# Batch 0 of a sparse attention and MLP kernel: local q, k and v cast in flight, attended tiles normalised in pairs, first weights queued early

## The chip, the cores and the metric

One core of a Trainium2 chip. The metric is the device time of one execution in microseconds, median of several executions. Five engines work side by side: TensorE (matmuls), VectorE, ScalarE, GpSimd, and SyncE, which here only issues transfers. Loads issued by SyncE go through the "hardware queue" and keep their type; loads issued by GpSimd go through the "software queue" and here cast float32 to bf16 in flight.

## The reference

```python
def _attn_ref(q, k, v):                      # q, k, v: (8, 8, 576, 64) float32
    scores = scale * np.matmul(q, k.transpose(0, 1, 3, 2))
    rel = pos[:, None] - pos[None, :]
    mask_local = (rel >= 0) & (rel < 32)                       # heads 0 to 3
    mask_strided = (rel >= 0) & (pos[None, :] % 32 == pos[:, None] % 32)   # heads 4 to 7
    ...                                       # masked softmax over the keys
    return np.matmul(attn, v)

def _moe_ref(x, w_in, w_out):                # x: (4608, 512), w_in: (512, 2048), w_out: (2048, 512)
    h = x @ w_in
    sp = np.where(h > 20.0, h, np.log1p(np.exp(np.minimum(h, 20.0))))
    return ((h * np.tanh(sp)) @ w_out).astype(np.float32)
# reference: x is the attention output, its heads side by side
```

## The kernel before

The parts that the change and the argument touch, with cuts. Heads 0 to 3 are called local, 4 to 7 strided. An "attended tile" is the attention output of 96 queries (local) or 72 (strided) for four heads. A "block" is 512 rows of x going through the MLP: its first half multiplies by w_in, its second by w_out. A "gate" is a tiny transfer on SyncE's queue; what is behind it is asked for only after the gate's source is written.

```python
# helpers: hardware queue (issued by SyncE) in float32, software queue (issued by GpSimd) casting to bf16
def load_qk_loc(b):                           # local k, q: 96 partitions x 6 rows, hardware queue
    for dst, src in ((kl32, k), (ql32, q)):
        nc.sync.dma_start(...)
def load_v_loc(b): ...                        # local v: 5 loads of 256-byte rows, hardware queue
def load_w_in(c0, c1):                        # 512 columns of w_in each, cast in flight
    for c in range(c0, c1):
        nc.gpsimd.dma_start(...)

# the prologue: attention of batch 0, cut
load_v_str(0); load_qk_loc(0); load_v_loc(0)
for p in P_s + P_l:
    Po.memset(p[:], 0.0)
...                                           # strided k, q: cast, transpose
cast(Po, vs[0][...], vs32[0:PN])
load_w_in(0, 1)
a.qk("s", 0, Dv); a.qk("s", 1, Dv, True)      # scores, exp, mask
cast_qk_loc(0, Dv, Po)
a.qk("s", 2, Dv, True)
load_w_in(1, 2)
...                                           # local v cast by Po; local k, q transposed; local scores
for j in range(8):
    a.pv("s", j)                              # attended tile, normalised alone by VectorE
a.mask("l", 2, Dv)
load_w_in(2, 4)
load_qk_str(1)
load_w_out(0, 2)
nc.sync.dma_start(gate[:], x_s[0:1, 5, :])    # SyncE's queue waits here, then asks for batch 1
load_qk_loc(1)
load_v(1)
...
cast_qk_loc(1, Po, Po)                        # GpSimd, in this order
cast_v(1, Po, Po)
load_w_out(2, 4)
load_qk_str(2)
for t in range(NBLK):                         # block t: MLP half 1 and transposes of batch t+1,
    ...                                       # then MLP half 2 and attention of batch t+1
            if t == 0:
                for n in {3: (4, 5), 4: (6, 7), 6: (0, 1), 7: (2, 3)}.get(i, ()):
                    ts[n]()                   # 0 to 3: strided k, q; 4 to 7: local k, q of batch 1
```

The softmax here doesn't subtract the row's maximum and nothing guards it: scores larger than these inputs give would overflow.

Of the kernel before, what the change touches and what calls it, by code (L numbers as in the profile page):

```python
# [37 lines left out]
def kernel(ctx, tc, q, k, v, moe_w_in, moe_w_out, out):  # L38
# [52 lines left out]
    def tile_t(name):  # L91
        return ps_t.tile([128, 512], F32, tag="pt", name=name)
# [8 lines left out]
    def load_qk_loc(b):  # L101
        for dst, src in ((kl32, k), (ql32, q)):
            nc.sync.dma_start(
                dst[0:PL].rearrange("p h j d -> p h (j d)"),
                src[b, 0:4].rearrange("h (p j) d -> p h (j d)", j=CL),
            )
# [30 lines left out]
    def cast(eng, out_, in_):  # L137
        if eng is nc.scalar:
            nc.scalar.copy(out_, in_)  # L139
        else:  # L140
            eng.tensor_copy(out_, in_)  # L141
# [11 lines left out]
    def t_step(b, kind, which, hp, eng=None):  # L153
# [13 lines left out]
        else:  # L167
# [10 lines left out]
                tr[:, 0:S].rearrange("c (j p) -> c p j", j=CL),  # L178
            )

    T_ORDER = [(kd, w, hp) for kd in ("s", "l") for hp in range(2) for w in ("k", "q")]

    def t_steps(b):
# [7 lines left out]
    class Attn:  # L191
# [40 lines left out]
                op=ALU.mult,  # L232
            )

        def pv(self, kind, i):
            po = tile_t("po")[:, 0:4 * (D + 1)].rearrange("p (h d) -> p h d", h=4)
            for h in range(4):
                if kind == "l":
                    n, m, rhs = 128, WQ, vl[self.b % 2][:, i, h, :]
                    pt, c0 = P_l[i // 2][:, h % 2], WQ * (2 * (h // 2) + i % 2)  # L240
                else:
                    n, m, rhs = PN, PN, vs[self.b % 2][0:PN, h, i, :]
                    job, u = S_AT[i // 2, h]
                    pt, c0 = P_s[job][:, i % 2], PN * u
                nc.tensor.matmul(  # L245
                    po[:, h, :], lhsT=pt[0:n, c0:c0 + 128], rhs=rhs,
                    start=True, stop=True,
                )
            dst = (x_l if kind == "l" else x_s)[0:m, i, :]
            rden = small.tile([128, 4], F32, tag="rden", name="rden")  # L250
            nc.vector.reciprocal(rden[0:m, :], po[0:m, :, D])  # L251
            nc.vector.tensor_tensor(  # L252
                out=dst.rearrange("p (h d) -> p h d", h=4), in0=po[0:m, :, 0:D],
                in1=rden[0:m, :].unsqueeze(2).to_broadcast([m, 4, D]), op=ALU.mult,
            )

        def xt(self, kind, hf, eng=None):
# [52 lines left out]
    def mlp1(t):  # L310
        gT = g_pool.tile([128, 16, 512], BF16, tag="gT", name="gT")

        def group(g):
            ps = ps_mm.tile([128, 2, 512], F32, tag="mm", name="psh")
            for u in range(2):
                fc = 2 * g + u
                for a, n, o in segs(t):
                    for cc in range(4):
                        nc.tensor.matmul(  # L319
                            ps[:, u, o:o + n], lhsT=w_in[:, cc, fc * 128:(fc + 1) * 128],  # L320
                            rhs=xT[:, cc, a:a + n], start=(cc == 0), stop=(cc == 3),
                        )
            nc.scalar.activation(gT[:, 2 * g:2 * g + 2, :], ps[:], AF.Mish)  # L323
        return gT, [lambda g=g: group(g) for g in range(8)]

    def mlp2(t, gT, fc_major=False):
# [22 lines left out]
    with tc.manual_schedule():  # L349
        Po, Dv, Sc = nc.gpsimd, nc.vector, nc.scalar  # L350
        Sc.preload_act_table(AF.Exp)
        Sc.dma_start(consts[:], consts_h.ap())
        st0 = []
        for src in (k, q):
            st = g_pool.tile([128, 16, 512], BF16, tag="gT", name="st0")
            st = st[:].rearrange("p a b -> p (a b)").bitcast(F32)[0:PN, 0:4 * CS * D]
            st = st.rearrange("p (h x) -> p h x", h=4)
            for hp in range(2):
                h = 2 * hp
                nc.sync.dma_start(  # L360
                    st[:, h:h + 2, :],
                    src[0, 4 + h:6 + h].rearrange("h (p j) d -> p h (j d)", j=CS),
                )
            st0.append(st)
        load_v_str(0)
        load_qk_loc(0)
        load_v_loc(0)
        Dv.memset(kTs[:, 16 * PN:16 * PN + 64], 0.0)
        Dv.memset(kTl[:, :, 0:32], 0.0)
        Dv.memset(vl32[0:32, 0, :, :], 0.0)  # L370
# [2 lines left out]
            Dv.memset(vl[i][:, :, :, D:D + 1], 1.0)  # L373
        for i in range(2):
            Dv.memset(vl[i][0:32, 0, :, D:D + 1], 0.0)
        for p in P_s + P_l:
            Po.memset(p[:], 0.0)

        a = Attn(0)
        for hp in range(2):  # L380
            h = 2 * hp
            cast(Dv, ks[0][0:PN, h:h + 2, :], st0[0][:, h:h + 2, :])
            t_step(0, "s", "k", hp, Dv)
        cast(Dv, qs[0][0:PN, 0:2, :], st0[1][:, 0:2, :])
        t_step(0, "s", "q", 0, Sc)
        cast(Sc, qs[0][0:PN, 2:4, :], st0[1][:, 2:4, :])
        t_step(0, "s", "q", 1, Sc)
        cast(Po, vs[0][0:PN, :, :, 0:D], vs32[0:PN])
        load_w_in(0, 1)
        a.qk("s", 0, Dv)  # L390
        a.qk("s", 1, Dv, True)
        cast_qk_loc(0, Dv, Po)
        a.qk("s", 2, Dv, True)
        load_w_in(1, 2)
        for i in range(0, NW, 3):
            cast(Po, vl[0][:, i:i + 3, :, 0:D], vl32[:, i:i + 3, :, :])
        for hp in range(2):
            t_step(0, "l", "k", hp, Dv)
            t_step(0, "l", "q", hp, Sc)
        a.qk("l", 0, Po)  # L400
        a.qk("l", 1, Po, True)
        a.qk("l", 2, None, True)
        for j in range(8):
            a.pv("s", j)
        a.mask("l", 2, Dv)
        load_w_in(2, 4)
        load_qk_str(1)
        load_w_out(0, 2)
        nc.sync.dma_start(gate[:], x_s[0:1, 5, :])
        load_qk_loc(1)  # L410
        load_v(1)
        for i in range(3):
            a.pv("l", i)
        a.xt("s", 0)
        a.xt("s", 1)
        for i in range(3, 6):
            a.pv("l", i)
        a.xt("l", 0)
        a.xt("l", 1)
        cast_qk_loc(1, Po, Po)  # L420
        cast_v(1, Po, Po)
        load_w_out(2, 4)
# [5 lines left out]
            load_v(2)  # L428

        for t in range(NBLK):  # L430
            gT, g1 = mlp1(t)
            ts = t_steps(t + 1) if t + 1 < B else []
            at = attn_steps(t + 1) if t + 1 < B else []
            if t == 0:
                at[8].append(load_next)
            for i, g in enumerate(g1):
                g()
                if t == 0:
                    for n in {3: (4, 5), 4: (6, 7), 6: (0, 1), 7: (2, 3)}.get(i, ()):
                        ts[n]()  # L440
                elif i < len(ts):
                    ts[i]()
            if t + 3 < B:
                load_qk_str(t + 3)
            for i, g in enumerate(mlp2(t, gT, fc_major=(t == 0))):
                g()
                if i < len(at):
                    for s in at[i]:
                        s()
            if t + 2 < B:  # L450
                cast_qk_loc(t + 2, Po, Po)
                cast_v(t + 2, Po, Po)
            if t + 3 < B:
                load_qk_loc(t + 3)
                load_v(t + 3)
# [30 lines left out]
```

## Time and profile before

| | before |
|---|---|
| time, median (range) of three executions | 348.3 us (347.7 to 348.6) |
| span in the profile | 345.9 us |
| TensorE busy | 315.6 us, 91% |
| first MLP matmul | 34.28 us |
| second half of block 0 starts | 51.99 us |
| block 1 starts | 72.15 us |
| each later block | 35.45 us |

The page of a kernel gives busy times, a picture of 40 equal slices in tenths, and groups of instructions. The chain of waits follows the last instruction back to what released it, step by step (start, duration, what). A timeline lists one engine's instructions: start, duration, engine, line, operation, what it writes and reads, and in square brackets how long the engine had been idle and on what. "PE" is TensorE, "POOL" GpSimd, "SPq" SyncE's queue. In the names, `kl`, `ql`, `vl` are local k, q, v, `ks`, `qs`, `vs` strided ones, `lq` the new bf16 buffer of batch 0's local k and q, `psh` and `pso` the results of the MLP's two halves. The lines that carry the reading are in the prediction below.

Two lines more are wanted later: on GpSimd's timeline of the kernel before, batch 1's local k and q are cast as they land.

```profile
32.11 1.46 POOL L141 CAST kl<-kl 96x1536 bf16<-96x1536 f32 x1 [0.19 <-DMA kl<-in_k_dram]
...
37.42 1.47 POOL L141 CAST ql<-ql 96x1536 bf16<-96x1536 f32 x1 [3.85 <-DMA ql<-in_q_dram]
```

Local k landed about 32.1 us and local q at 37.4, with TensorE needing them after 42 us.

### The profile page before, as it was taken

How to read it: one execution, taken by the hardware profiler on the slowest of the kernel's cores; microseconds unless marked ns; L12 is line 12 of the kernel's file. 1: busy time of each engine (PE TensorE's matmuls, PEld its weight loads, DVE VectorE, ACT ScalarE, POOL GpSimd, SP SyncE). 2: the span in 40 equal slices, each digit the busy share in tenths (PEclk: the TensorE clock that was granted, in tenths of full speed). 3: DMA queues.
4: the chain of work that ended last, by engine and by line, in shares of the span. 5: the costliest groups of instructions: out<-in, count | busy, mean ns of one | idle time of the engine just before them, and what ended most of it. 6: DMA issues, size and time to landing. Idle time of an engine off the chain costs nothing.

```text
span 345.9 us, 6447 instructions
## 1 busy us (share of the span) xinstructions
PE 315.6 (91%) x2737; PEld 171.2 (49%) x2784; DVE 115.3 (33%) x315; ACT 174.8 (51%) x191; POOL 116.1 (34%) x101
## 2 busy tenths in 40 slices
PE   1366999999999999999999999999999999999993
PEld 1244454555455545554569655544555454444441
DVE  3356044523462236233632363236423540000000
ACT  1543447275646464656465645665466637414511
POOL 5368215726292109310941086007700600000000
PEclk9999999999999999999999999999999999999999
DMA  6997993999993961299119810960110011011011
GB/s 182 206 172 175 225 178 59 189 214 245 223 198 92 227 106 62 64 221 140 63 41 246 138 37 27 244 110 1 63 63 0 2 63 61 0 63 61 0 63 61
DMA packets 48573, 39.63 MB, mean 115 GB/s; under 512 B 26656, under 2 KB 41056, under 8 KB 48544
## 3 DMA queue, kind: packets, MB, share of 16 engines
q1 hardware_dynamic: 38576, 30.81, 38.7%
q0 software_dynamic: 9824, 8.33, 15.3%
q8 instruction: 22, 0.36, 0.5%
q10 hardware_dynamic: 144, 0.08, 0.1%
q14 instruction: 7, 0.06, 0.1%
HBM read 38.09 MB, written 9.44 MB: 137 GB/s over the span
## 4 chain that ended last, share of the span: by engine, by line
PE 72%; DMA 8%; SPq 5%; DVE 5%; issue 3%; ACT 3%; POOL 3%; POOLq 0%; ACTq 0%
PE psh L319 32%; PE pso L334 28%; PE po L245 4%; DMA ql<-in_q_dram 4%; DMA vl<-in_v_dram 4%; SPq L117 4%; DVE x_s L252 2%; PE tr L170 2%; PE tr L161 2%; PE ps L202 2%; ACT Ps L220 2%; DVE qTl L141 1%; PE ps L213 1%; PE trx L275 1%; PE trx L265 1%
## 5 line engine op out<-in xcount | busy, mean ns | idle before, releaser
L334 PE MATMUL pso<-w_out,gT 128*128 128x512 bf16 x546 | 136.9, 379 | 1.5 <-issue 0.2
L319 PE MATMUL psh<-xT,w_in 128*128 128x512 bf16 (+1 forms) x623 | 134.0, 360 | 1.8 <-ACT xT L139 0.7
L323 ACT ACTIVATE gT<-psh 128x1024 bf16<-128x1024 f32 x72 | 73.7, 1024 | 56.0 <-PE psh L319 54.6
L319 PEld LDWEIGHTS <-w_in 128*128 128x128 bf16 x640 | 60.3, 99 | 55.5 <-issue 3.6
L334 PEld LDWEIGHTS <-gT 128*128 128x128 bf16 x576 | 49.0, 97 | 44.3
L139 ACT COPY xT<-trx 128x576 bf16<-128x576 bf16 x32 | 20.4, 639 | 47.8 <-PE trx L275 31.8
L229 POOL TENSOR_TENSOR Ps<-Ps,consts_sb 72x576 bf16<-72x576 bf16 x7 | 8.9, 1275 | 90.0 <-ACT Ps L220 90.0
L229 POOL TENSOR_TENSOR Pl<-Pl,consts_sb 128x768 bf16<-128x768 bf16 x23 | 37.1, 1641 | 1.4 <-ACT Pl L220 1.3
L341 ACT COPY osb<-pso 128x1024 f32<-128x1024 f32 x18 | 18.2, 1012 | 27.4 <-PE pso L334 27.4
L251 DVE RECIPROCAL rden<-po 72x4 f32<-72x4 f32 (+1 forms) x112 | 19.8, 176 | 36.5 <-PE po L245 36.4
L252 DVE TENSOR_TENSOR x_s<-po,rden 72x256 bf16<-72x256 f32 x64 | 26.9, 420 | 2.2
L220 ACT ACTIVATE Pl<-ps 128x768 bf16<-128x768 f32 x24 | 19.2, 811 | 14.0 <-PE ps L202 14.0
L220 ACT ACTIVATE Ps<-ps 72x864 bf16<-72x864 f32 (+1 forms) x24 | 19.1, 806 | 7.4 <-PE ps L213 6.6
L141 DVE COPY kTl<-tr 128x576 bf16<-128x576 bf16 x16 | 12.1, 758 | 29.8 <-PE tr L170 29.8
L252 DVE TENSOR_TENSOR x_l<-po,rden 96x256 bf16<-96x256 f32 x48 | 20.2, 421 | 1.7
L141 POOL CAST vs<-vs 72x2048 bf16<-72x2048 f32 x8 | 15.2, 1896 | 12.9 <-DMA vs<-in_v_dram 12.9
L229 DVE TENSOR_TENSOR Ps<-Ps,consts_sb 72x864 bf16<-72x864 bf16 (+1 forms) x17 | 10.6, 622 | 26.3 <-ACT Ps L220 26.3
L141 DVE COPY kTs<-tr 128x576 bf16<-128x576 bf16 x16 | 7.3, 458 | 34.8 <-PE tr L161 34.8
L245 PE MATMUL po<-vs,Ps 72*128 72x65 bf16 x256 | 17.2, 201 | 1.8 <-DVE x_s L252 0.9
L141 POOL CAST vl<-vl 128x768 bf16<-128x768 f32 x16 | 12.8, 831 | 15.1 <-DMA vl<-in_v_dram 15.1
L245 PE MATMUL po<-vl,Pl 128*128 128x65 bf16 x192 | 14.6, 200 | 3.3 <-DVE rden L251 2.5
L245 PEld LDWEIGHTS <-Ps 72*128 72x128 bf16 x256 | 12.2, 101 | 8.4 <-DVE x_s L252 3.7
(47 smaller groups left out, 211.1 us busy)
## 6 DMA issues: line engine op xcount, KB each, us to landing
out_dram<-osb SPq DMA_DIRECT2D x18, 512.0 KB, 3.1
vl<-in_v_dram SPq DMA_DIRECT2D x32, 160.0 KB, 9.2
vs<-in_v_dram SPq DMA_DIRECT2D x8, 576.0 KB
kl<-in_k_dram SPq DMA_DIRECT2D x8, 576.0 KB, 8.4
ql<-in_q_dram SPq DMA_DIRECT2D x8, 576.0 KB, 8.5
w_in<-in_moe_w_in_dram POOLq DMA_DIRECT2D x4, 512.0 KB, 8.7
w_out<-in_moe_w_out_dram POOLq DMA_DIRECT2D x4, 512.0 KB, 14.5
ks<-in_k_dram POOLq DMA_DIRECT2D x7, 288.0 KB, 12.1
```

What stands on the lines that cost most here:

```text
L117: nc.sync.dma_start(vl32[:, 1:NW, h, :], win)
L139: nc.scalar.copy(out_, in_)
L141: eng.tensor_copy(out_, in_)
L220: nc.scalar.activation(pt[0:n, :, 0:nw], ps[0:n, :, 0:nw], AF.Exp, scale=scale)
L229: meng.tensor_tensor(out=pm, in0=pm, in1=mk[0:n, :].unsqueeze(1).unsqueeze(1).to_broadcast([n, 2, nu, w]), op=ALU.mult,)
L245: nc.tensor.matmul(po[:, h, :], lhsT=pt[0:n, c0:c0 + 128], rhs=rhs, start=True, stop=True,)
L251: nc.vector.reciprocal(rden[0:m, :], po[0:m, :, D])
L252: nc.vector.tensor_tensor(out=dst.rearrange("p (h d) -> p h d", h=4), in0=po[0:m, :, 0:D], in1=rden[0:m, :].unsqueeze(2).to_broadcast([m, ...
L319: nc.tensor.matmul(ps[:, u, o:o + n], lhsT=w_in[:, cc, fc * 128:(fc + 1) * 128], rhs=xT[:, cc, a:a + n], start=(cc == 0), stop=(cc == 3),)
L323: nc.scalar.activation(gT[:, 2 * g:2 * g + 2, :], ps[:], AF.Mish)
L334: nc.tensor.matmul(p[:, ot % 2, :], lhsT=gT[:, fc, 128 * ot:128 * ot + 128], rhs=w_out[:, fc, :], start=(fc == 0), stop=(fc == 15),)
L341: nc.scalar.copy(osb[:], p[:])
```

## The change

Its intent is to start the MLP earlier. Local q, k and v of batch 0 are cast by the transfer and no longer by engines; q and k go to partitions 64 to 127. All four chunks of w_in are queued right behind them. VectorE normalises two attended tiles at a time. The first two groups of the MLP begin with the half of their contraction that is ready first. The gate for batch 1 now waits for the third chunk of w_in, and the transposes of batch 1 move later: the local ones by two groups, one of the strided ones by one.

```diff
+    def t_step_loc0(src, dst, hp, eng):       # 64x64 transposes from partitions 64 to 127
+        tr = tile_t("tr")[:].bitcast(BF16)
+        for j in range(9):
+            for e in range(2):
+                nc.tensor.transpose(
+                    tr[64 * e:64 * e + 64, 64 * j:64 * j + 64], src[64:128, 2 * hp + e, j, :],
+                    ident[64:128, 64:128],
+                )
+        cast(eng, ...)
 ...
+        def pv2(self, kind, i, from_mm=False): # two attended tiles, one reciprocal, one multiply
+            po = tile_s(from_mm)[:, :, 0:4 * (D + 1)].rearrange("p e (h d) -> p e h d", h=4)
+            for e in range(2):
+                self.pv_mm(kind, i + e, po[:, e])
+            ...
 ...                                           # mlp1(0): groups 0 and 1 split in two halves of the contraction
-        load_qk_loc(0)
-        load_v_loc(0)
-        for p in P_s + P_l:
+        for p in P_s:
+            Dv.memset(p[:], 0.0)
+        for p in P_l[0:2]:
             Po.memset(p[:], 0.0)
+        load_loc0(kl0, k)                      # Po.dma_start: cast in flight
+        Po.memset(P_l[2][:], 0.0)
+        load_loc0(ql0, q)
+        Po.dma_start(vl[0][32:128, 0, :, 0:D], ...)
+        for h in range(4):
+            Po.dma_start(vl[0][:, 1:NW, h, 0:D], win)
+        load_w_in(0, 4)
 ...
-        load_w_in(0, 1)  / load_w_in(1, 2) / load_w_in(2, 4), cast_qk_loc(0, ...), casts of vl
-        for j in range(8):
-            a.pv("s", j)
+        a.pv2("s", 0) ... a.pv2("s", 2, True) ... a.pv("s", 4); a.pv("s", 5) ... a.pv2("s", 6)
         load_qk_str(1)
         load_w_out(0, 2)
-        nc.sync.dma_start(gate[:], x_s[0:1, 5, :])
+        nc.sync.dma_start(gate[:], w_in[0:1, 0, 1024:1280])
 ...
-                    for n in {3: (4, 5), 4: (6, 7), 6: (0, 1), 7: (2, 3)}.get(i, ()):
+                    for n in {5: (4, 5), 6: (6, 7, 0), 7: (1, 2, 3)}.get(i, ()):
```

More of the change, by code (lines that the diff above doesn't have):

```diff
@@ L179, in t_step @@
             )
+    def t_step_loc0(src, dst, hp, eng):
[6 more added lines that the diff above has]
+                )
+        cast(
+            eng, dst.rearrange("c (p j) -> c p j", j=9),
+            tr[:, 0:S].rearrange("c (j p) -> c p j", j=9),
+        )
     T_ORDER = [(kd, w, hp) for kd in ("s", "l") for hp in range(2) for w in ("k", "q")]
@@ L233, in mask, with pv_mm @@
             )
-        def pv(self, kind, i):
-            po = tile_t("po")[:, 0:4 * (D + 1)].rearrange("p (h d) -> p h d", h=4)
+        def pv_mm(self, kind, i, po):
             for h in range(4):
                 if kind == "l":
-                    n, m, rhs = 128, WQ, vl[self.b % 2][:, i, h, :]
+                    n, rhs = 128, vl[self.b % 2][:, i, h, :]
                     pt, c0 = P_l[i // 2][:, h % 2], WQ * (2 * (h // 2) + i % 2)
                 else:
-                    n, m, rhs = PN, PN, vs[self.b % 2][0:PN, h, i, :]
+                    n, rhs = PN, vs[self.b % 2][0:PN, h, i, :]
                     job, u = S_AT[i // 2, h]
@@ L248, in pv @@
                 )
+        def pv(self, kind, i):
+            po = tile_t("po")[:, 0:4 * (D + 1)].rearrange("p (h d) -> p h d", h=4)
+            m = WQ if kind == "l" else PN
+            self.pv_mm(kind, i, po)
             dst = (x_l if kind == "l" else x_s)[0:m, i, :]
@@ L254, in pv @@
                 in1=rden[0:m, :].unsqueeze(2).to_broadcast([m, 4, D]), op=ALU.mult,
+            )
+        def pv2(self, kind, i, from_mm=False):
+            po = tile_s(from_mm)[:, :, 0:4 * (D + 1)].rearrange("p e (h d) -> p e h d", h=4)
+            m = WQ if kind == "l" else PN
+            for e in range(2):
+                self.pv_mm(kind, i + e, po[:, e])
+            dst = (x_l if kind == "l" else x_s)[0:m, i:i + 2, :]
+            rden = small.tile([128, 2, 4], F32, tag="rden2", name="rden2")
+            nc.vector.reciprocal(rden[0:m], po[0:m, :, :, D])
+            nc.vector.tensor_tensor(
+                out=dst.rearrange("p e (h d) -> p e h d", h=4), in0=po[0:m, :, :, 0:D],
+                in1=rden[0:m].unsqueeze(3).to_broadcast([m, 2, 4, D]), op=ALU.mult,
             )
@@ L311, in mlp1, with group @@
         gT = g_pool.tile([128, 16, 512], BF16, tag="gT", name="gT")
-        def group(g):
-            ps = ps_mm.tile([128, 2, 512], F32, tag="mm", name="psh")
+        held = {}
+        def group(g, ccs=(2, 3, 0, 1)):
+            if g not in held:
+                held[g] = ps_mm.tile([128, 2, 512], F32, tag="mm", name="psh")
+            ps = held[g]
             for u in range(2):
@@ L317, in group @@
                 for a, n, o in segs(t):
-                    for cc in range(4):
+                    for cc in ccs:
                         nc.tensor.matmul(
                             ps[:, u, o:o + n], lhsT=w_in[:, cc, fc * 128:(fc + 1) * 128],
-                            rhs=xT[:, cc, a:a + n], start=(cc == 0), stop=(cc == 3),
+                            rhs=xT[:, cc, a:a + n], start=(cc == 2), stop=(cc == 1),
                         )
-            nc.scalar.activation(gT[:, 2 * g:2 * g + 2, :], ps[:], AF.Mish)
+            if ccs[-1] == 1:
+                nc.scalar.activation(gT[:, 2 * g:2 * g + 2, :], ps[:], AF.Mish)
+        if t == 0:
+            return gT, [lambda g=g, c=c: group(g, c) for c in ((2, 3), (0, 1)) for g in range(2)] + [
+                lambda g=g: group(g) for g in range(2, 8)
+            ]
         return gT, [lambda g=g: group(g) for g in range(8)]
@@ L352 @@
         Sc.dma_start(consts[:], consts_h.ap())
-        st0 = []
-        for src in (k, q):
-            st = g_pool.tile([128, 16, 512], BF16, tag="gT", name="st0")
-            st = st[:].rearrange("p a b -> p (a b)").bitcast(F32)[0:PN, 0:4 * CS * D]
-            st = st.rearrange("p (h x) -> p h x", h=4)
-            for hp in range(2):
-                h = 2 * hp
+        st0 = g_pool.tile([128, 16, 512], BF16, tag="gT", name="st0")
+        st0 = st0[:].rearrange("p a b -> p (a b)").bitcast(F32)[0:PN]
+        st0 = [st0[:, 2048 * i:2048 * i + 2048].rearrange("p (h x) -> p h x", h=4) for i in range(2)]
+        for st, src in zip(st0, (k, q)):
+            for h in (0, 2):
                 nc.sync.dma_start(
@@ L363, with load_loc0 @@
                 )
-            st0.append(st)
         load_v_str(0)
-        load_qk_loc(0)
-        load_v_loc(0)
+        lq0 = g_pool.tile([128, 16, 512], BF16, tag="gT", name="lq0")
+        lq0 = lq0[:].rearrange("p a b -> p (a b)")
+        kl0, ql0 = [
+            lq0[:, 2304 * i:2304 * i + 2304].rearrange("p (h j d) -> p h j d", h=4, j=9) for i in range(2)
+        ]
+        def load_loc0(dst, src):
+            Po.dma_start(
+                dst[64:128].rearrange("p h j d -> p h (j d)"),
+                src[0, 0:4].rearrange("h (p j) d -> p h (j d)", j=9),
+            )
         Dv.memset(kTs[:, 16 * PN:16 * PN + 64], 0.0)
@@ L375 @@
             Dv.memset(vl[i][0:32, 0, :, D:D + 1], 0.0)
-        for p in P_s + P_l:
+        Dv.memset(vl[0][0:32, 0, :, 0:D], 0.0)
+        for p in P_s:
+            Dv.memset(p[:], 0.0)
+        for p in P_l[0:2]:
             Po.memset(p[:], 0.0)
+        load_loc0(kl0, k)
+        Po.memset(P_l[2][:], 0.0)
+        load_loc0(ql0, q)
+        Po.dma_start(vl[0][32:128, 0, :, 0:D], v[0, 0:4, 0:96, :].rearrange("h p d -> p h d"))
+        for h in range(4):
+            win = bass.AP(
+                v.tensor, v[0, h:h + 1, WQ - 32:WQ, :].offset, [[D, 128], [WQ * D, NW - 1], [1, D]]
+            )
+            Po.dma_start(vl[0][:, 1:NW, h, 0:D], win)
+        load_w_in(0, 4)
         a = Attn(0)
@@ L382 @@
             cast(Dv, ks[0][0:PN, h:h + 2, :], st0[0][:, h:h + 2, :])
-            t_step(0, "s", "k", hp, Dv)
-        cast(Dv, qs[0][0:PN, 0:2, :], st0[1][:, 0:2, :])
-        t_step(0, "s", "q", 0, Sc)
-        cast(Sc, qs[0][0:PN, 2:4, :], st0[1][:, 2:4, :])
-        t_step(0, "s", "q", 1, Sc)
-        cast(Po, vs[0][0:PN, :, :, 0:D], vs32[0:PN])
-        load_w_in(0, 1)
-        a.qk("s", 0, Dv)
-        a.qk("s", 1, Dv, True)
-        cast_qk_loc(0, Dv, Po)
-        a.qk("s", 2, Dv, True)
-        load_w_in(1, 2)
-        for i in range(0, NW, 3):
-            cast(Po, vl[0][:, i:i + 3, :, 0:D], vl32[:, i:i + 3, :, :])
-        for hp in range(2):
-            t_step(0, "l", "k", hp, Dv)
-            t_step(0, "l", "q", hp, Sc)
-        a.qk("l", 0, Po)
-        a.qk("l", 1, Po, True)
-        a.qk("l", 2, None, True)
-        for j in range(8):
-            a.pv("s", j)
-        a.mask("l", 2, Dv)
-        load_w_in(2, 4)
+            t_step(0, "s", "k", hp, Sc)
+        for hp in range(2):
+            h = 2 * hp
+            cast(Dv, qs[0][0:PN, h:h + 2, :], st0[1][:, h:h + 2, :])
+            t_step(0, "s", "q", hp, Sc)
+            t_step_loc0(kl0, kTl[:, hp, 32:32 + S], hp, Sc)
+        cast(Dv, vs[0][0:PN, :, :, 0:D], vs32[0:PN])
+        for i in range(3):
+            a.qk("s", i, Dv if i < 2 else None, i > 0)
+        for hp in range(2):
+            t_step_loc0(ql0, qTl[:, hp, :], hp, Sc)
+        a.pv2("s", 0)
+        a.mask("s", 2, Dv)
+        a.qk("l", 0, None, True)
+        a.pv2("s", 2, True)
+        a.mask("l", 0, Dv)
+        a.pv("s", 4)
+        a.pv("s", 5)
+        a.qk("l", 1, Po, True)
+        a.qk("l", 2, Po, True)
+        a.pv2("s", 6)
         load_qk_str(1)
         load_w_out(0, 2)
-        nc.sync.dma_start(gate[:], x_s[0:1, 5, :])
+        nc.sync.dma_start(gate[:], w_in[0:1, 0, 1024:1280])
         load_qk_loc(1)
         load_v(1)
-        for i in range(3):
-            a.pv("l", i)
+        gT, g1 = mlp1(0)
         a.xt("s", 0)
         a.xt("s", 1)
-        for i in range(3, 6):
-            a.pv("l", i)
+        a.pv2("l", 0)
+        a.pv2("l", 2, True)
+        g1[0]()
+        a.pv("l", 4)
+        a.pv("l", 5)
         a.xt("l", 0)
+        g1[1]()
         a.xt("l", 1)
+        g1 = g1[2:]
         cast_qk_loc(1, Po, Po)
@@ L430 @@
         for t in range(NBLK):
-            gT, g1 = mlp1(t)
+            if t > 0:
+                gT, g1 = mlp1(t)
             ts = t_steps(t + 1) if t + 1 < B else []
```

## The prediction

> **What bounds the kernel now.** I read the page's rows first, then the chain of waits up to 75 us, then GpSimd's timeline across the one long transfer on that chain, then stretches by engine, then the DMA queues by window. From the page of the kernel before:
>
> ```profile
> span 345.9 us, 6447 instructions
> PE 315.6 (91%) x2737; PEld 171.2 (49%) x2784; DVE 115.3 (33%) x315; ACT 174.8 (51%) x191; POOL 116.1 (34%) x101
> ...
> PE   1366999999999999999999999999999999999993
> ...
> DMA  6997993999993961299119810960110011011011
> ```
>
> TensorE is idle for 345.9 - 315.6 = 30.3 us, nearly all in the first four of 40 slices (8.65 us each): the attention of batch 0, before any MLP matmul can run. The timeline puts the first MLP matmul at 34.28 us, the first matmul of the second MLP half of block 0 at 51.99, and the start of block 1 at 72.15. After that a block takes 107.74 - 72.29 = 35.45 us, and the next 35.45 again, at TensorE's pace. Only the time before 72.15 can shrink. The DMA row is full there as well, but for a gap just before slice 4. The stretches say the same:
>
> ```profile
> 34.00:52.00 18.00, 17.39 (x118) 8.76 (x121) 3.73 (x7) 9.01 (x10) 3.36 (x2) 1.00 1.15 203
> 52.00:72.20 20.20, 19.09 (x206) 10.03 (x207) 10.61 (x32) 10.40 (x13) 11.95 (x12) 1.00 0.82 137
> ...
> 89.80:107.70 17.90, 17.21 (x184) 9.32 (x187) 9.25 (x30) 8.94 (x12) 12.30 (x9) 1.00 0.85 156
> ```
>
> (columns: PE, PEld, DVE, ACT, POOL busy, clock, DMA share, GB/s). The second half of block 0 takes 20.2 us where block 1's takes 17.9: something holds TensorE up by some 2 us. The chain of waits names it:
>
> ```profile
> 27.15 0.57 SPq L103
> ...
> 37.67 4.31 SPq L117
> 42.02 13.27 DMA vl<-in_v_dram
> 55.43 0.94 POOL vl L141 x2
> ```
>
> So what sets the end is not the late start of the MLP. It is the local v of batch 1, requested behind k and q of batch 1 from 27.15 us on and complete at about 55.4. GpSimd, whose queue is in order, is stuck behind it:
>
> ```profile
> 55.43 1.60 POOL L141 CAST vl<-vl 128x768 bf16<-128x768 f32 x2 [10.82 <-DMA vl<-in_v_dram]
> 56.98 1.50 POOL L132 DMA_DIRECT2D w_out<-in_moe_w_out_dram  x2
> 58.45 0.76 POOL L97 DMA_DIRECT2D ks<-in_k_dram  x1
> 59.17 0.75 POOL L97 DMA_DIRECT2D qs<-in_q_dram  x1
> ...
> 61.30 1.32 POOL L229 TENSOR_TENSOR Ps<-Ps,consts_sb 72x576 bf16<-72x576 bf16 x1
> ```
>
> After the cast it issues six loads, and only at 61.30 masks the last strided scores of batch 1. The mask ends at 62.62, 7.2 us after the landing. TensorE's next attention product starts at 62.67, and block 0 ends 9.5 us later. There are thus two chains into 72.15: the MLP's start plus its work, and the landing of v plus 7.2 + 9.5 = 16.7 us.
>
> **What the Trainium skill says.** "DMA: Bandwidth & Descriptors", section "Issuing engines are not separate DMA queues": loads issued by any engine run on the same 16 DMA engines and interleave. The trace agrees: from 28 to 55.4 us the software queue takes 58.8% of the engines and the hardware queue 41.7%, 100.5% together. Moving a load from SyncE to GpSimd makes no bandwidth. The same page, "SWDGE vs HWDGE vs iDMA": a cast in flight needs a load issued from GpSimd, which is why the local loads move there; here too all casting loads are on the software queue. "SBUF — State Buffer", section "Who interferes with whom": VectorE in a two-port mode and GpSimd block each other. The first 72x1024 cast, beside GpSimd's memset, took 1.35 us, the next ones 0.68: it agrees. "TensorE: Matmul & The Clock Gate", section "Wait — 56ns, not 53.3ns?": a 512-wide matmul every 427 ns cold, 216 ns warm. Block 0's first matmuls start about 0.42 us apart and eight warm ones take 1.73 us: it agrees.
>
> **The change part by part.**
>
> *Casts.* Gone for batch 0: kl on VectorE 0.95 us, ql on GpSimd 1.57, vs on GpSimd 1.89 (moved to VectorE, estimated 1.4 from 0.68 for half its columns), vl on GpSimd 1.60. The wait for ql (landed about 17.2, cast to 18.9) opens the old chain, so its removal counts for the start.
>
> *Transposes.* Local q and k now have nine rows a partition and 64x64 transposes: 4 x 18 = 72 in place of 4 x 6 = 24. At 0.66/8 = 0.083 us (the eight 72x72 ones) that is 1.5 us a step against 0.66, so 3.3 us more of TensorE, mostly while it waits for data.
>
> *Normalising in pairs.* A tile costs 0.18 + 0.42 = 0.60 us of VectorE, one after another for strided tiles (23.02 to 27.6). A pair should cost about 0.2 + 0.7 = 0.9 (a cast's slope is (0.95 - 0.68)/512 = 0.53 ns a column; I take twice that for PSUM in float32). Five pairs and four single tiles come to 6.9 us in place of 14 x 0.6 = 8.4: 1.5 us off a chain that carries it, and fewer handovers.
>
> *Masks and memsets.* GpSimd gives three memsets (2.6 us) to VectorE, which has gaps, and keeps the masks of local jobs 1 and 2.
>
> *Start of the MLP.* Walking it through: strided v lands about 14 (12.4 before, but local k and q now share the engines), its cast ends 15.4, two masks 16.6, the pairs and single tiles with their masks about 22.5, transposes and local pairs 25 to 26, the last transposes and copies 28 to 30. The first eight matmuls have then already run in between. I take 29.5, and with 8 x 0.216 = 1.7 us done early and about 1 us of cold matmuls moved into the gap, the lead is 34.28 - 29.5 + 1.7 + 1.0 = about 7.5 us.
>
> *The DMA chain.* Work before, as share times window: 2.5 to 25 us at 102.5% is 23.1 us, and 28 to 55.4 at 100.5% is 27.5; together 50.6. Between lies a gap of about 3.5 us, in which the w_in loads had not been issued. The change queues all w_in behind batch 0 and fills the gap. Per packet the trace shows about 100 ns for the hardware queue's kl and ql (768 of 1536 bytes: 4.8 us of 16 engines) and 98 ns for casting ones of w_in (2048 bytes read). Local k and q in flight are 2 x 256 packets of 2304 bytes: at 110 ns, 3.5 us, saving 1.3. Local v keeps its 2944 packets of 256 bytes (about 25 ns, 4.6 us); as casting packets of 128 bytes written they may cost that or up to 40 ns, 2.8 us more. I take +1. Total about 50.3 us, at 102.5% 49.1 us, from 2.5 us on: the last load lands at about 51.5. A check from the other side: the third w_in chunk, which now opens the gate for batch 1, should land at 26 to 28. Batch 1 took 28.3 us behind the gate before, with 2.69 MB on the software queue; now 0.52 MB of that has already passed, some 4 us. So 27 + 24.3 = 51.3.
>
> *Sum.* Local v of batch 1 lands at about 51.2 instead of 55.4, 4.2 earlier. The path behind it (16.7 us) is unchanged: same cast, six issues, mask. Block 0 ends at 67.9 by this chain and at 72.15 - 7.5 = 64.7 by the MLP's. The later wins, with perhaps 0.3 us from TensorE's being further ahead when the mask ends: the gain is 4.5 us.
>
> **The rivals.**
>
> *The start decides alone* (v of batch 1 hidden): the gain would be about 7.5 us, 341. For it: the local transposes of batch 1 are moved two groups later, so the author saw late data. Against: the in-order chain of GpSimd at 55.43, and a DMA row with no air to pull v forward by more than its gap.
>
> *Casting small packets are dear.* If local v costs 40 to 50 ns a packet or GpSimd blocks on its descriptor space with eleven loads at once, the gate opens near 30, v lands near 54, and the gain is 1 to 2 us: 346.5. For it: 128-byte writes appear nowhere in this trace. Against: six loads in a row (27.37 to 31.9) issued at 0.75 us each without blocking.
>
> *Contention slows the front*: strided q and v wait behind local k and q, 72 small transposes run cold, and the MLP starts at 32. Then both chains give about 4 us: 344.5. *A new early stall*: the gate moves from x_s (26.46) to w_in; were it at 32, batch 1 would come later than now, and the time would be 348 to 350.
>
> **Range and chances.** 348.3 - 4.5 = 343.8 us. Low, 340.5: DMA lands v by 48 and the start's lead of 7.5 counts in full. High, 346.8: dear small packets. Faster by over 2% needs 341.35 or less, so nearly the whole lead: 0.18. Within 2%: 0.79. Slower by 2%: 0.03; steady blocks are not touched.
>
> **What would show it.** Right: first full MLP group near 29 to 30 us; DMA row full from 3 to 50 us without the gap at 25 to 28; local v of batch 1 landing at 50 to 52.5; GpSimd again idle before that cast; TensorE waiting for the mask of the third strided job by several us in the second half of block 0; later blocks still 35.45 us. Wrong: that landing below 48, no TensorE wait at the mask, a gate later than 29, or casting packets of local v well over 30 ns each.

## The result, and the profile after

The changed kernel took 345.04 us (344.87 to 345.23 in four executions) against 348.07 us for the kernel before beside it, a ratio of 0.9912 with a 95% interval of 0.9895 to 0.9929. A ratio is the mean time of one kernel's executions over that of the other's in the same rounds, so it is not quite the ratio of the medians. Executions over 1.5% slower than the fastest of the same kernel are left out of the means. The time lies within the predicted range and within 2%, as was held most likely. The gain is 3.0 us and not 4.5. The way it comes about, however, is not the predicted one.

The page of the changed kernel:

```profile
span 343.1 us, 6523 instructions
PE 315.6 (92%) x2784; PEld 171.8 (50%) x2832; DVE 113.8 (33%) x306; ACT 175.8 (51%) x194; POOL 114.9 (33%) x101
...
PE   1688689999999999999999999999999999999993
...
PEclk9999989999999999999999999999999999999999
DMA  7999959999915931397129811940010011011011
```

The front is fuller, but the fifth slice (34 to 43 us) has a hole that was not there before: TensorE falls to 6 tenths, and in the slice after it its clock dips to 8. The chain of waits of the changed kernel says why (cut):

```profile
25.95 1.45 SPq L103
...
27.46 12.99 DMA ql<-in_q_dram
...
40.50 1.47 POOL ql L141
...
42.02 0.66 PE tr L170 x6
42.68 3.06 PE psh L355 x8
```

The chain goes through local **q** of batch 1, not through local v. GpSimd's timeline of the changed kernel shows all of it:

```profile
24.01 0.79 POOL L97 DMA_DIRECT2D ks<-in_k_dram  x1
...
37.02 1.46 POOL L141 CAST kl<-kl 96x1536 bf16<-96x1536 f32 x1 [9.97 <-DMA kl<-in_k_dram]
40.50 1.46 POOL L141 CAST ql<-ql 96x1536 bf16<-96x1536 f32 x1 [2.02 <-DMA ql<-in_q_dram]
...
47.19 1.60 POOL L141 CAST vl<-vl 128x768 bf16<-128x768 f32 x2 [1.20 <-DMA vl<-in_v_dram]
...
55.58 1.27 POOL L243 TENSOR_TENSOR Ps<-Ps,consts_sb 72x576 bf16<-72x576 bf16 x1 [2.49 <-ACT Ps L234]
```

Local v of batch 1 landed at 47.2 us, 8 earlier than before, and the mask behind it waits for ScalarE and no longer for GpSimd's queue. Local k and q landed 5 and 3 us **later** than before, although they were asked for 1.2 us earlier. TensorE, some 7 us ahead by then, stood still for them: 2.7 us by the list of waits. It then ran its next eight matmuls in 3.06 us where eight take 1.73; the granted clock was 0.58 in this stretch (42.68 to 45.74 us).

Where the time went, from the starts of the stages in the two timelines of TensorE. First the kernel before:

```profile
34.28 0.59 PE L319 MATMUL psh<-xT,w_in 128*128 128x512 bf16 x1 [0.73 <-ACT xT L139]
...
51.99 1.03 PE L334 MATMUL pso<-w_out,gT 128*128 128x512 bf16 x4
...
72.15 1.89 PE L319 MATMUL psh<-xT,w_in 128*128 128x512 bf16 x8
```

and the changed kernel:

```profile
29.66 1.89 PE L355 MATMUL psh<-xT,w_in 128*128 128x512 bf16 x8 [0.73 <-ACT xT L139]
...
42.02 0.66 PE L170 MATMUL tr<-consts_sb,ql 96*128 96x96 bf16 x6 [2.71 <-POOL ql L141]
...
50.06 1.03 PE L375 MATMUL pso<-w_out,gT 128*128 128x512 bf16 x4
...
69.47 1.89 PE L355 MATMUL psh<-xT,w_in 128*128 128x512 bf16 x8
```

| stage | before | after | gain |
|---|---|---|---|
| MLP of block 0 starts | 34.28 | 29.66 | 4.6 |
| first half of block 0 | 17.7 | 20.4 | -2.7 |
| second half of block 0 | 20.2 | 19.4 | 0.8 |
| block 1 starts | 72.15 | 69.47 | 2.7 |
| span | 345.9 | 343.1 | 2.8 |

The first half should have become shorter, since eight of its matmuls were done before it began. The 0.8 us gained in the second half match TensorE's wait for GpSimd's masks in the kernel before (0.5 and 0.3 us), which is gone.

### The profile page after: what moved, and what is told of

Read it like the earlier page. It is cut to its first block, busy times and chain, and to the rows that moved or that the text cites. A ratio compares the mean times of both kernels' runs of the same rounds, so it can differ in the third digit from the quotient of the medians.

```text
span 343.1 us, 6523 instructions
## 1 busy us (share of the span) xinstructions
PE 315.6 (92%) x2784; PEld 171.8 (50%) x2832; DVE 113.8 (33%) x306; ACT 175.8 (51%) x194; POOL 114.9 (33%) x101
## 3 DMA queue, kind: packets, MB, share of 16 engines
q0 software_dynamic: 13392, 9.30, 20.2%
## 4 chain that ended last, share of the span: by engine, by line
PE 77%; DMA 10%; DVE 4%; issue 3%; ACT 3%; POOL 1%; SPq 1%; ACTq 0%; POOLq 0%
PE psh L355 33%; PE pso L375 30%; PE po L258 4%; DMA ql<-in_q_dram 4%; DMA lq<-in_q_dram 3%; DMA w_in<-in_moe_w_in_dram 3%; PE tr L161 2%; PE tr L170 2%; DVE x_s L270 2%; PE ps L216 2%; ACT Ps L234 2%; PE ps L227 1%; DVE qTl L141 1%; PE trx L307 1%; PE trx L297 1%
## 5 line engine op out<-in xcount | busy, mean ns | idle before, releaser
L269 DVE RECIPROCAL rden<-po 72x4 f32<-72x4 f32 (+1 forms) x102 | 18.0, 177 | 33.6 <-PE po L258 33.6
L270 DVE TENSOR_TENSOR x_s<-po,rden 72x256 bf16<-72x256 f32 x58 | 24.4, 421 | 2.0
L141 DVE COPY kTl<-tr 128x576 bf16<-128x576 bf16 x14 | 10.6, 757 | 31.3 <-PE tr L170 31.3
L270 DVE TENSOR_TENSOR x_l<-po,rden 96x256 bf16<-96x256 f32 x44 | 18.5, 421 | 1.5
L141 DVE COPY qTl<-tr 128x576 bf16<-128x576 bf16 x14 | 10.6, 757 | 17.4 <-PE tr L170 17.4
L141 DVE COPY kTs<-tr 128x576 bf16<-128x576 bf16 x14 | 6.4, 456 | 29.3 <-PE tr L161 29.3
L141 POOL CAST kl<-kl 96x1536 bf16<-96x1536 f32 x7 | 10.2, 1459 | 16.8 <-DMA kl<-in_k_dram 16.8
L258 PE MATMUL po<-vs,Ps 72*128 72x65 bf16 x232 | 14.6, 197 | 0.1
L258 PE MATMUL po<-vl,Pl 128*128 128x65 bf16 x176 | 12.9, 197 | 1.8 <-DVE rden L269 1.8
```

The costliest lines, as they stand in the source:

```text
L141: eng.tensor_copy(out_, in_)
L258: nc.tensor.matmul(po[:, h, :], lhsT=pt[0:n, c0:c0 + 128], rhs=rhs, start=True, stop=True,)
L269: nc.vector.reciprocal(rden[0:m, :], po[0:m, :, D])
L270: nc.vector.tensor_tensor(out=dst.rearrange("p (h d) -> p h d", h=4), in0=po[0:m, :, 0:D], in1=rden[0:m, :].unsqueeze(2).to_broadcast([m, ...
```

## The experiments

**Theory A**: the lead at the start is lost because local q of batch 1 lands late; and it lands late because its request stands behind a backlog on the software queue (the last w_in chunk, strided k and q of batch 1, half of w_out). **Theory B**, the prediction's: local v of batch 1 and GpSimd's mask set the end. **Theory C**: the start of the MLP alone sets it. Each run was timed in five rounds beside the kernel before, and all gave correct results. The runs "after_again", "latew", "before_earlyw" and "front" ran on another chip than the rest of the experiments.

### gate1: the gate on the second chunk of w_in

```diff
-        nc.sync.dma_start(gate[:], w_in[0:1, 0, 1024:1280])
+        nc.sync.dma_start(gate[:], w_in[0:1, 0, 512:768])
```

> The changed kernel, but the load of batch 1's local k and q waits for the second chunk of w_in instead of the third. Theory A (the lead at the start is lost because TensorE waits 2.7 us for the transposes of local q of batch 1, which landed at 40.5 us, and then runs cold): q lands about 3 us earlier, near 37.5, the wait shrinks below 0.5 us, the time falls by 2.5 to 4 us to about 342. Theory B (local v of batch 1 and GpSimd's mask set the end, as predicted before the run): little earlier v, gain under 1 us, about 344.5. Theory C (the start of the MLP alone sets it): unchanged at 345.0, or worse through contention.

Measured: 341.03 us, ratio 0.9791 (0.9775 to 0.9807). Local q was cast at 35.7 us and TensorE did not wait for it. The MLP began at 29.67 us, as in the changed kernel, so theory C fails. Now the predicted wait shows, on TensorE's timeline of this run:

```profile
56.46 0.30 PE L258 MATMUL po<-vs,Ps 72*128 72x65 bf16 x4 [0.62 <-POOL Ps L243]
```

Local v landed at 49.2 us here, the mask ended at 56.4, and block 1 began at 65.91, which is 9.5 us later: the prediction's second chain, with its own interval. Theory A holds, and B is the next bound behind it, worth 0.6 us here.

### order: strided transposes of batch 1 first, no transfer moved

```diff
-                    for n in {5: (4, 5), 6: (6, 7, 0), 7: (1, 2, 3)}.get(i, ()):
+                    for n in {5: (0, 1), 6: (2, 3), 7: (4, 5, 6, 7)}.get(i, ()):
```

> The changed kernel, but in the first half of block 0 the strided transposes of batch 1 come first and the local ones last. No transfer is moved. Theory A: the strided k and q have landed by 39 us, so the 2.7 us wait and the cold matmuls behind it vanish: 341.5 to 342.5. Theory B (v and mask of batch 1): no change, 345.0. Should the strided q of batch 1 land after 40 us the wait only changes its name: 344 to 345.

Measured: 340.17 us (339.77 to 340.84), ratio 0.9772 (0.9758 to 0.9787), faster than was expected. Local q was still cast only at 40.1 us, but TensorE's list of waits has no wait for it:

```profile
PE psh L355 <- ACT xT L139: 0.7, 1, 0.7
PE tr L170 <- DVE kTl L141: 0.6, 1, 0.6
PE psh L355 <- ACT gT L360: 0.4, 1, 0.4
PE po L258 <- POOL Pl L243: 0.3, 1, 0.3
```

(who waited for whom, us in total, times, longest). The MLP began at 29.28 us, its first half took 15.9 us, and block 1 began at 64.68:

```profile
64.68 1.89 PE L355 MATMUL psh<-xT,w_in 128*128 128x512 bf16 x8
```

That is a lead of 7.5 us over the kernel before. So the wait for local q, with what followed it, cost 20.4 - 15.9 = 4.5 us of the first half, and that is the difference between a lead of 7.5 and a gain of 3.0. This one edit, which moves no byte, is the clearest proof of A.

### single: the pairs undone in the changed kernel

```diff
-        a.pv2("s", 0)
+        a.pv("s", 0)
+        a.pv("s", 1)
 ...                       # and so at the other four places
```

> The changed kernel with the pairs undone: every attended tile normalised alone again. Theory A: VectorE needs some 1.5 us more before the MLP starts (near 31), but the wait for local q of batch 1 swallows it: 345.0 plus or minus 0.5. Theory C (the start counts in full): 346.5.

Measured: 342.92 us, ratio 0.9844 (0.9827 to 0.986): two microseconds **faster** than the changed kernel, which no theory had. The MLP began at 32.15 us, 2.5 later, and yet block 1 began at 67.53, 1.9 us earlier. GpSimd, later too, issued strided k of batch 1 at 25.97 us, and SyncE had asked for local k at 25.30, just ahead of it. In the changed kernel it is 24.01 and 25.95, the other way round. Local k was cast at 31.9 and q at 34.9 us, and TensorE had no wait for them. The order of two requests on two queues matters; how far it alone decides is looked at under "hwfirst".

### hwfirst: the software queue's loads behind local k and q

```diff
-        load_qk_str(1)
-        load_w_out(0, 2)
         nc.sync.dma_start(gate[:], w_in[0:1, 0, 1024:1280])
 ...
         cast_qk_loc(1, Po, Po)
+        load_qk_str(1)
+        load_w_out(0, 2)
```

> The changed kernel, but the casting loads of strided k, q of batch 1 and of the first half of w_out are issued after the casts of local k and q of batch 1, so these have the DMA engines nearly alone. Theory A, with the reason that the software queue's backlog delays local k and q: k lands within 6 us of its request (11 us now), q near 34, no wait at the local transposes; the strided k and q may then come late instead. Time 342 to 344. If k still takes about 11 us to land, the backlog is not the reason.

Measured: 341.7 us, ratio 0.9809 (0.9784 to 0.9834), just under the expected range. Local k was asked for at 26.21 us, a little later than in the changed kernel, and landed before 31.5: 5.3 us instead of 11. Local q was cast at 34.0. The DMA queues between 26 and 31 us (packets, MB, share of the 16 engines), first of the changed kernel:

```profile
q0 software_dynamic: 892, 0.77, 109.3%
...
q1 hardware_dynamic: 32, 0.00, 0.7%
```

and of this run:

```profile
q1 hardware_dynamic: 574, 0.81, 69.5%
q0 software_dynamic: 110, 0.10, 12.4%
```

In the changed kernel the hardware queue moved 32 packets in these 5 us, and at 0.00 MB they are not local k's 1536-byte ones (in the kernel before, too, 32 such packets go with the gate); its first packets of local k come between 31 and 32 us, some 5.5 us after the request. Here they come between 27 and 28, about a microsecond after it. The backlog is the reason for the late k and q. TensorE now waited 0.5 us for w_out instead.

Over the runs, local k took this long from its request to its landing: 5.3 us with none of the moved loads ahead ("hwfirst"), 5.0 to 7.5 where it was asked for before strided k (the kernel before, "order_qkhw", "single", "order_gate1", "gate1"), and 8.0, 9.1, 10.3 and 11.1 us where it came 0.4, 1.1, 2.0 and 1.9 us behind it ("order_single", "after_again", "order", the changed kernel). "front" does not fit, with 8.6 us at 3.5 us behind: the order of the requests is not the whole of it.

### after_again: the changed kernel once more

No edit.

> The changed kernel itself, on one chip with the runs beside it: 345.0 plus or minus 0.6, and local q of batch 1 again landing near 40 us with a TensorE wait of some 2.7 us. If it is near 343 instead, the gain of the run with the pairs undone was chance of the chip.

Measured: six executions at 340.91, 341.06, 344.79, 345.02, 345.52 and 347.11 us, median 344.91; the last counts as slow and the ratio, 0.9874 (0.983 to 0.9918), leaves it out. The changed kernel has two outcomes, and the first measurement had met only the long one. The mean granted clock goes with them: 0.996 and 0.999 in the two short executions, 0.991 to 0.994 in the three near 345. The profiled execution was a short one, span 339.1 us. GpSimd's timeline of it:

```profile
34.14 1.46 POOL L141 CAST kl<-kl 96x1536 bf16<-96x1536 f32 x1 [7.22 <-DMA kl<-in_k_dram]
38.07 1.47 POOL L141 CAST ql<-ql 96x1536 bf16<-96x1536 f32 x1 [2.47 <-DMA ql<-in_q_dram]
```

and its chain of waits (cut):

```profile
25.62 12.39 DMA ql<-in_q_dram
...
38.07 1.48 POOL ql L141
...
40.02 1.73 PE psh L355 x8
```

Local k was asked for at 25.00 us here and 25.95 in the long execution, 1.1 and 1.9 us behind the first of the software loads. Its first packets came between 28 and 29 us. TensorE waited 1.2 us instead of 2.7, stayed at full clock (eight matmuls in 1.73 us and not 3.06), and block 1 began at 65.47 instead of 69.47. Of these 4.0 us, 0.9 are an earlier start, 1.5 the wait and 1.3 the clock. Same code, same data: the rest of theory A is seen without an edit. That the clock fell because of the longer wait is inferred: of the two profiles, the one with 2.7 us of wait shows it, the one with 1.2 does not. My expectation, 345.0 plus or minus 0.6, was a miss for the profiled execution, though the median lies in it; and the gains of "gate1", "single" and "hwfirst" over the changed kernel are gains over its long outcome only; "order" lies some 0.8 us under the short one. That they are not luck is seen from the counts: seven of the nine fast executions of the changed kernel were long, and none of the 17 of "gate1", "order", "single" and "hwfirst". Why the third w_in chunk lands a microsecond sooner in some executions stays open.

### latew: the early weights undone in the changed kernel

```diff
-        load_w_in(0, 4)
+        load_w_in(0, 2)
 ...
+        load_w_in(2, 4)
         load_qk_str(1)
 ...
-        nc.sync.dma_start(gate[:], w_in[0:1, 0, 1024:1280])
+        nc.sync.dma_start(gate[:], x_s[0:1, 5, :])
```

> The changed kernel with the early weights undone: half of w_in early, the other half behind the local masks, and the gate on the fifth strided tile as in the kernel before. Theory (local k and q of batch 1 come late because their requests stand behind the software queue's backlog): the gate opens near 21.5 us, ahead of the software loads, k lands before 30, the TensorE wait for local q is gone: 341 to 343, faster than the changed kernel. Rival (the early weights pay): TensorE waits for the last chunk of w_in instead, which lands near 40 us: 345 or more.

Measured: 345.13 us, ratio 0.9921 (0.9908 to 0.9933). The transfers did what A says: asked for at 21.8 us, local k was cast at 28.8 and q at 31.4. The time did not follow. TensorE's list of waits in this run:

```profile
PE psh L355 <- DMA w_in<-in_moe_w_in_dram: 1.8, 1, 1.8
PE po L258 <- POOL Ps L243: 1.6, 1, 1.6
```

The rival was right that the weights come too late, and the prediction's chain is back as well: local v at 51.2 us, mask from 57.5 to 58.8, block 1 at 68.31, again 9.5 us behind the mask. So the early weights, with the later gate that goes with them, are worth nothing against the long outcome of the changed kernel (345.0) and some 4 us against its short one (341.0): what they gain is lost again where local k and q come late.

### before_earlyw: the kernel before with the early weights alone

```diff
         for p in P_s + P_l:
             Po.memset(p[:], 0.0)
+        load_w_in(0, 4)
 ...                       # and the three later load_w_in taken out
```

> The kernel before with one part of the change alone: all four w_in chunks issued right after the memsets. If the software queue's backlog starves the hardware queue, on which local k, q and v of batch 0 still come: v of batch 0 lands near 30 us instead of 22.5, the MLP starts later than 34.28 and the time is 350 to 356. If queuing the weights early fills the gap in the DMA row for nothing, as the prediction's sum of DMA work has it: 345 to 347.

Measured: 353.38 us, ratio 1.0167 (1.0151 to 1.0182), as expected. Local v of batch 0, on the hardware queue, could be cast only at 29.47 us instead of 22.56, and the MLP began at 39.95. The weights may go first only because the change has moved the loads of batch 0 to the same queue, ahead of them.

### order_single, order_qkhw, order_vhw: what the parts are worth once the wait is gone

These start from the run "order". The pairs undone, as above:

> The run with strided transposes first, and the pairs undone. With the wait for local q of batch 1 out of the way a later start of the MLP must show. In the earlier run with the pairs undone the MLP started at 32.15 us instead of 29.28. If the start now sets the end: 340.2 plus 2 to 3 us, 342 to 343. If batch 1's v and GpSimd's masks set it (they cost TensorE 0.3 us here): 340.2 to 341.

Measured: 342.45 us, ratio 0.9832 (0.9818 to 0.9845), as expected. The MLP began at 32.3 us. The ratios differ by 0.006, some 2.1 us: the pairs count in full now, more than the 1.5 us that VectorE's durations had given.

Local q and k of batch 0 by the hardware queue, with the old casts and transposes:

```diff
         load_v_str(0)
+        load_qk_loc(0)
 ...
-        load_loc0(kl0, k)
-        load_loc0(ql0, q)
 ...
+        cast_qk_loc(0, Dv, Po)
-            t_step_loc0(ql0, qTl[:, hp, :], hp, Sc)      # and the two for kl0
+            t_step(0, "l", "k", hp, Sc)
+            t_step(0, "l", "q", hp, Sc)
```

> The run with strided transposes first, but batch 0's local q and k come in float32 on the hardware queue behind strided v, with the casts and 96-partition transposes of the kernel before. If the cast in flight is what made the earlier start: the MLP starts 2 to 4 us later, 342 to 344. If the early weights and pairs made it: within 1 us of 340.2.

Measured: 344.67 us, ratio 0.9901 (0.9887 to 0.9914), above both expectations. The MLP began at 33.85 us. The cast in flight of q and k, with the queue and the transposes that go with it, is worth 0.013 of the time before, some 4.5 us, with the rest of the change in place.

Local v of batch 0 by the hardware queue, with GpSimd's cast behind the issues of w_in:

```diff
         load_v_str(0)
+        load_v_loc(0)
 ...
-        Po.dma_start(vl[0][32:128, 0, :, 0:D], ...)      # and the four others
         load_w_in(0, 4)
+        for i in range(0, NW, 3):
+            cast(Po, vl[0][:, i:i + 3, :, 0:D], vl32[:, i:i + 3, :, :])
```

> The run with strided transposes first, but batch 0's local v is loaded in float32 on the hardware queue and cast by GpSimd as before the change. Its casting packets took 54 ns each where the prediction had 25 to 40. If they hold the front up: third chunk of w_in lands 2 us earlier, start of the MLP no later, time 339 to 340.5. If the cast in flight was worth its place: GpSimd waits for v before the local masks, start up to 2 us later, 341 to 343.

Measured: 349.43 us, ratio 1.0034 (1.0014 to 1.0054), outside both expectations. GpSimd's timeline of it:

```profile
4.36 3.50 POOL L125 DMA_DIRECT2D w_in<-in_moe_w_in_dram  x4
29.92 1.60 POOL L141 CAST vl<-vl 128x768 bf16<-128x768 f32 x2 [22.06 <-DMA vl<-in_v_dram]
```

All w_in went out at once, and v on the other queue landed at 29.9 us. I had weighed only the cost of its small packets, and had not applied the backlog, just shown for local k and q, to v. By this run v's part is worth 9 us, more than the whole gain: the parts need each other, and their worths do not add up.

### order_gate1: both mends together

The edits of "order" and "gate1".

> The run with strided transposes first, and the gate on the second chunk of w_in. If the wait for local q was the only loss the two mends are worth the same gain once: 340 to 341, nothing added. If they added up, 337. The masks of batch 1 may wait for local v, which landed at 49.2 us under the earlier gate against 47.7: then 340.5 to 341.5.

Measured: 341.24 us, ratio 0.9802 (0.9786 to 0.9818): nothing added to "order" (0.9772), rather a little lost. Local k and q came at 29.9 and 35.3 us, but now the strided q of batch 1 and the mask made TensorE wait 0.7 and 0.5 us. The two mends remove the same wait, and an earlier gate only hands the engines from one load to another.

### front: "order" with the strided scores of batch 0 ahead of the local transposes

```diff
             t_step(0, "s", "q", hp, Sc)
-            t_step_loc0(kl0, kTl[:, hp, 32:32 + S], hp, Sc)
-        cast(Dv, vs[0][0:PN, :, :, 0:D], vs32[0:PN])
         for i in range(3):
             a.qk("s", i, Dv if i < 2 else None, i > 0)
+        cast(Dv, vs[0][0:PN, :, :, 0:D], vs32[0:PN])
+        for hp in range(2):
+            t_step_loc0(kl0, kTl[:, hp, 32:32 + S], hp, Sc)
```

> The run with strided transposes first, and in the front of batch 0 both strided q transposes and the three strided score jobs ahead of the local transposes, so that TensorE does not wait 2.9 us for local k before them, with the cast of strided v behind the first two masks. If local k's landing holds the front: the MLP starts about 1 us earlier, 339 to 340. If the landing of strided v (14.6 us) holds it: unchanged, 340.2.

Measured: 339.38 us (338.49 to 339.51), ratio 0.9751 (0.9738 to 0.9763), the lowest of all. The MLP began at 28.73 us, 0.55 earlier than in "order", and block 1 at 64.07. It is 2.5% under the kernel before and beats the changed kernel in both its outcomes (340.91 us at the least, in the same session); against "order", timed in another session, the intervals still overlap a little, so the last step is likely, not certain.

## Why the prediction was right or wrong, point by point

- **The start of the MLP**: 29.5 us predicted, 29.66 measured. **The lead**, 7.5 us with the eight early matmuls: "order", where nothing takes it back, has 6.8 us at the end of the first half (51.99 - 45.21) and 7.5 at block 1 (72.15 - 64.68); the last 0.7 came in the second half, where the kernel before waited 0.8 us for the masks and "order" 0.3. Right to within 0.7 us, though by balancing errors: the pairs were sized too small (1.5 us for some 2.1), and the 72 small transposes too dear. Eighteen of them took 0.69 us against a predicted 1.5, so the feared 3.3 us more of TensorE did not exist.
- **What held the kernel before**: misread. The prediction compared block 0's second half (20.2 us) with 17.9 us of block 1, but its window began at 89.8, and block 1's second half begins at 88.05: it takes 19.7 us. So the half was held up by some 0.5 us and not 2; TensorE's list of waits for it has 0.8 us for GpSimd's masks. The chain of v was thus barely binding before the change. Nor did nearly all of TensorE's 30.3 us of idle time lie before the MLP: 18.9 of them did.
- **"The DMA chain"**: this is the step that failed. Its sum let local v of batch 1 land at about 51.2 us; it landed at 47.2. The sum took the DMA share times time as a measure of work with a ceiling near 102.5%. Between 13 and 22 us the changed kernel shows 176% for the software queue alone: packets of one engine overlap in time there, and their shares add up beyond the engines. From 2.5 to 47.2 us the two queues' shares come to 122.9%, that is 54.9 us of such work where the sum had 50.3: neither its work nor its ceiling held. The check from the other side counted all 28.3 us behind the gate, though the last of them were no full load (the hardware queue's share from 53 to 56 us was 14%).
- **"The later wins"**: so the chain of v did not set the end. Three of the prediction's own signs of being wrong came true: v landed before 48 us, TensorE did not wait at the mask, and v's casting packets took well over 30 ns. Its own interval, 9.5 us from the mask's end to block 1, was right each time that this chain did bind (gate1: 56.40 to 65.91; latew: 58.80 to 68.31).
- **The gate**: predicted at 26 to 28 us, opened at 25.3. The prediction treated the time after it as one batch that arrives as a whole. It did not ask when the first members, local k and q, are needed by a TensorE that is 7 us ahead. That was the missing chain: they landed at 37.0 and 40.5 us, and cost 4.5 us in the long outcome.
- **Rivals**: dear small packets were half right: the software queue's packets, mostly local v's, took 54, 71 and 45 ns from 13 to 14, 14 to 15 and 15 to 16 us, above the predicted 25 to 40, but the gate did not move to 30. "A new early stall" named the right place, the loads of batch 1, with the wrong reason (a late gate) and the wrong sign of the total.
- **The number**: 343.8 predicted, 345.04 measured. A lead of 7.5 less a loss of 4.5 is 3.0; the prediction had 4.5 from a chain that was not there. That the number fell into the range is luck: a lead much as predicted, less a loss that nobody foresaw.

## What to carry to other kernels

Loads on two queues share the engines, but not always fairly in time: here a load asked for behind a long backlog on the other queue saw nothing move for some 5 us. When an engine is made to run ahead, list every input that it now meets earlier, not only the one that bound it before, and put first the work whose data is already there. If a gain depends on which of two queues is asked first, time the kernel often enough to see both outcomes.

## What the Trainium skill lacked or had wrong

- "DMA: Bandwidth & Descriptors", section "Queues, rings and completion order", says that each DMA engine takes the queues in turn, a packet at a time. It gives no time for how long a queue may stand. The runs show some 5.5 us from a request to its first packet behind a backlog on the software queue, and about 1 us without ("hwfirst"). Turns packet by packet alone would not lead one to expect that; what explains it, no run here shows.
- No page that I read says how many loads may be open on the software queue. Here the ninth of GpSimd's loads, the second w_in chunk, waited 2.2 us for the first, local k, to land, and the tenth for the second; in "order_qkhw", too, the ninth waited for the first, 2.8 us; without the five small loads of v ("order_vhw") four chunks went out in 3.5 us. This fits eight open loads; whether chip or compiler sets it stays open.
- "TensorE: Matmul & The Clock Gate", section "Part 4: PE-mode transpose", has times for 128x128 only. Here 18 transposes of 64x64, in turn to the two halves of the result's partitions, took 0.69 us, 38 ns each, while eight of 72x72 right behind them took 0.66 us, 83 ns each.
- "Perfetto Trace Analysis", section "Identifying the Most-Contended Engine", calls occupancy misleading for DMA because there are 16 engines. It does not say that the shares of packets add up beyond 100% of the 16: 176% over 9 us here, with 2317 of 3637 packets under 512 bytes, so a share is no measure of how much room is left.
